# Moving a tile's scaling behind the branch and ending the routing two steps earlier in layer 1 of a two-layer expert kernel

## The chip, the cores and the metric

The kernel runs on one core of one Trainium2 chip. The metric is device time in microseconds of one execution, the median of the runs shown. Engines are named as in the profile: PE is the matrix engine (PEld its weight loads), DVE, ACT and POOL are the vector, scalar and general engines, SP issues most DMAs.

## The reference, cut to what matters

An attention block (4 x 8 heads, 576 rows, head width 64) gives 2304 token rows of width 512. Two mixture-of-experts layers follow, each with 8 experts of 512 x 1024 x 512.

```python
x = attention(q, k, v, M_prev, z_prev, beta)          # 2304 x 512
# layer 1: one expert a token
logits = x @ w_gate + modality_bias[modality_id]
e_idx = argmax(logits); gate_w = softmax(logits)[e_idx]
out[mask] = gate_w[mask] * (relu(x[mask] @ w1[e]) @ w2[e])     # per expert
# layer 2: two experts a token, chosen from the output of layer 1
logits = x @ w_gate; noise_scale = log1p(exp(x @ w_noise))
noisy = logits + noise_scale * noise
top2, w = two largest of noisy, softmax over the two
out[mask] += w * (relu(x[mask] @ w1[e]) @ w2[e])                # per expert, twice a token
```

What matters below: layer 2's choice of experts (the routing) needs each output row of layer 1, and layer 1's rows must be multiplied by the gate weight (the scaling) before they are routed.

## The kernel before, in words

**Units.** Layer 1 works in units of 256 rows (two tiles of 128) that share one expert. A unit of the common kind is written by `full` (line 791). The number of units is known only on the chip, so the last ones, and the units of half-filled experts written by `pair` (line 828), stand in nested `If` blocks (lines 780 and 785): the next block is entered by a branch that falls through, and when the count is reached all engines jump to the code behind all blocks. In this data unit 0 is done together with the attention, then come full unit 1, one pair, and full units 2 to 8, and then layer 2. So there are two jumps: from the pair to unit 2, and from unit 8 to layer 2.

**Slots.** A full unit has 16 slots. In slots 0 to 7 (loop variable f) `mm1` makes 128 of the 1024 hidden columns: 12 matmuls of 256 columns (lines 712 to 714: each fp32 value is split into a high and a low part, and three products are added). ACT then writes `hh`, DVE `hl`. In slots 8 to 15 (t and q, i=4t+q) `mm2` makes the two output tiles: four slots of six matmuls of 512 columns for each tile (lines 722 to 724).

**Work that rides along.** In slots 0 to 7 the second weight is split (`split_w`, line 685: ACT writes the high part `w2h`, POOL or DVE subtracts for the low part `w2l`). In slots 7 to 14 the next unit's first weight is split in the same way (`split_w1`, line 689, `w1h` and `w1l`; POOL has columns 0, 1, 3, 5, 7 and DVE 2, 4, 6). `rows` transposes the next unit's gathered rows on PE (line 702, tile `gs`). `logits` makes layer 2's logits of the unit before.

**The routing chain.** `route2` (line 868) is a generator of some 35 small operations, most on DVE, that routes the 256 rows of the unit before. `pump(slot)` issues PUMP of them. The chain yields 1 behind `A` (line 899), the one-hot sum of the two chosen experts: from there it is held until slot GATE[1], where PE counts the rows by five small matmuls of `A` (lines 901 to 905). Behind them DVE works out the places (`rk`, `W`, `r`, `ri`, `col`, `ol`, `oc`), POOL copies weights into `val` (line 920), and DVE forms `rrm` (line 928); there the chain yields 2 and its last matmuls wait until slot 1 of the next unit (`behind`).

**The end of a unit.** ACT scales output tile 0 behind slot 11 and output tile 1 behind slot 15 (line 827, in a pair line 861) into `x1`. `settle` issues what is left of the chain up to its second hold, and `kept` (line 771) has POOL copy two small tables for the next unit's routing. `x1_out` (line 865) writes both tiles to memory.

The order of instructions on each engine is that of the code: inside these loops nothing else reorders them, and each engine works in order.

Of the kernel before, what the change touches and what calls it, by code (L numbers as in the profile page):

```python
# [9 lines left out]
FT=mybir.dt.float32; FR=mybir.dt.float32r; I32=mybir.dt.int32  # L10
AF=mybir.ActivationFunctionType; OP=mybir.AluOpType; AX=mybir.AxisListType
# [272 lines left out]
NF=13; NH=8; NP2=NH//2; NSTAT=5; COLS=2*NF+NH; SLOTS=COLS*128  # L284
HC=4; FC=HC+NH
col=lambda u: 2*u if u<2 else FC+2*(u-2)
# [5 lines left out]

EARLY=256; CH=(C2-DEAD)//2
OLP=8
LSLOT=(0,1,3); GATE={1:12,2:99}; PUMP=5
LSLOT2=(0,1,3); GATE2={1:7,2:11}; PUMP2=8
AREAS=(9216,9216,5120,10240,8192,GB*XW,2*XW,512)

# [9 lines left out]
class Moe:  # L308
# [420 lines left out]
    def state(s):  # L729
        nc=s.nc; c=s.c  # L730
        s.run=c.tile([128,E],FT,name='run'); nc.gpsimd.memset(s.run,float(DEAD))
        s.M2=c.tile([128,4,NC2],FT,name='M2'); nc.gpsimd.memset(s.M2,0.0)

        s.NV=NF+NP2+1
        s.sv=c.tile([128,s.NV,2,4],FT,name='sv'); nc.gpsimd.memset(s.sv,8000.0)
        s.val=c.tile([128,s.NV,4,4],FT,name='val'); nc.gpsimd.memset(s.val,0.0)
        s.nz=c.tile([128,3,2,E],FT,name='nz')
        s.L=c.tile([128,2,2*E],FT,name='L'); s.nx=c.tile([128,2,2],FT,name='nx'); s.nxi=c.tile([128,2],I32,name='nxi'); s.lp=c.tile([128,UT],FT,name='lp')
        s.uxi=c.tile([128,2,NF],I32,name='uxi'); s.cnt=c.tile([128,2],I32,name='cnt')
        s.last=c.tile([128,NF],FT,name='last')  # L740
        s.gn=c.tile([128,NF,2],FT,name='gn'); s.gh=c.tile([128,NP2+1,2],FT,name='gh'); s.gni=c.tile([128,NF,2],I32,name='gni')
        s.gsi=c.tile([128,NP2+1,2],I32,name='gsi')
# [32 lines left out]
        G.tensor_copy(s.nz[:,2,:nt],s.nz[:,1,:nt])  # L775
    def layer1(s, w1, w2, wcat):
        nc=s.nc; tc=s.tc; s.wcat=wcat; wk=s.wk; ps=s.ps
        s.full(wk,ps,w1,w2,1)
        s.np=nc.values_load(s.cnt[0:1,1:2],min_val=0,max_val=NP2)
        with ExitStack() as deep:  # L780
            for p in range(NP2):
                deep.enter_context(tc.If(s.np>p)); s.pair(wk,ps,w1,w2,p)
        for u in range(2,NSTAT): s.full(wk,ps,w1,w2,u)
        s.nf=nc.values_load(s.cnt[0:1,0:1],min_val=1,max_val=NF-1)
        with ExitStack() as deep:  # L785
            for u in range(NSTAT,NF):
                deep.enter_context(tc.If(s.nf>u-1)); s.full(wk,ps,w1,w2,u)
    def behind(s):

        for _ in s.old: pass  # L790
    def settle(s):

        while s.hold!=2: s.pump(99,{1:0,2:0},1)
        s.old=s.chain
    def full(s, wk, ps, w1, w2, u):
        nc=s.nc; V=nc.vector
        e=s.expert(1,0) if u==1 else s.expert(0,u-1); s.load_w(s.w1r,w1,e)
        s.x1_out(s.np*2+2 if u==2 else col(u-1),2)
        s.chain=s.route2(wk,ps,u-1,2); s.hold=0
        nc.gpsimd.tensor_copy(s.nz[:,1],s.nz[:,0])  # L800
        for f in range(KF):
            s.mm1(ps,f,0,UT)
            if u==1: s.late(f)
            elif f==1: s.behind()
            if u>=NSTAT-1:
                if f==1:
                    last=s.last[:,u-1:u]
                    V.tensor_scalar(s.nx[:,0],s.M2[:,0,0:2],float(S0),0.0,op0=OP.add,op1=OP.max)
                    V.tensor_scalar(s.nx[:,1],s.nx[:,0],float(N),last,op0=OP.add,op1=OP.mult)
                    V.tensor_add(s.nxi,s.nx[:,1],s.gn[:,u-1])  # L810
                    V.tensor_scalar(s.run[:,0:1],last,float(EARLY),s.run[:,0:1],op0=OP.mult,op1=OP.max)
                if f==2: g=[s.gather(s.xd[:N+col(u-1)*128],s.nxi[:,t:t+1]) for t in range(2)]
            elif f==(7 if u==1 else 0): g=[s.gather(s.xd[:N],(s.gsi[:,0] if u==1 else s.gni[:,u-1])[:,t:t+1]) for t in range(2)]
            if f in LSLOT: s.logits(wk,ps,1+LSLOT.index(f))
            s.split_w(s.w2r,s.w2h,s.w2l,f,nc.vector if f in (3,5,7) else nc.gpsimd)
            if f>LSLOT[2]: s.pump(f)
            if f==7: s.split_w1(0,nc.gpsimd)
        s.load_w(s.w2r,w2,e)
        for t in range(2):
            for q in range(4):  # L820
                y=s.mm2(ps,t*128,range(2*q,2*q+2),y if q else None)
                i=4*t+q
                if i<7: s.split_w1(i+1,nc.vector if i%2 else nc.gpsimd)
                if i in ((3,5) if u==1 else (1,3)): s.rows(ps,i//4 if u==1 else i//2,g[i//4 if u==1 else i//2],s.xf[0] if u==1 else None)
                if t==1 and q==1: s.logits(wk,ps,0)
                s.pump(8+i)
            nc.scalar.activation(s.x1[:,t,:D],y,AF.Copy,scale=s.gws[:,col(u)+t:col(u)+t+1])
        s.settle()
        s.kept(col(u),2)
    def pair(s, wk, ps, w1, w2, p):  # L830


        nc=s.nc; V=nc.vector; G=nc.gpsimd; c0=HC+2*p
        e=s.expert(1,p+1); eb=s.expert(1,NP2+1+p)
        s.load_w(s.wb1,w1,eb)
        s.x1_out(c0-2,2)
        s.load_w(s.wb2,w2,eb)
        s.chain=s.route2(wk,ps,NF+p,2); s.hold=0
        G.tensor_copy(s.nz[:,1],s.nz[:,0])
        xf=s.xf[p%2]; g=[]  # L840
        for t,(a1,a2) in enumerate(((s.w1r,s.w2r),(s.wb1,s.wb2))):
            cs=slice(t*128,t*128+128)
            for q in range(4):
                if q%2==0: h=ps.tile([128,4,128],FT,name='h')
                for f in (2*q,2*q+1):
                    for k in range(KD): nc.tensor.matmul(h[:,f%4],a1[:,k,f*128:f*128+128],xf[:,k,cs],start=k==0,stop=k==KD-1)
                if q%2: nc.scalar.activation(s.hf[:,2*q-2:2*q+2,cs],h,AF.Relu)
                if t==0:
                    if q==1: s.behind(); g=[s.gather(s.xd[:N],s.gsi[:,p+1,j:j+1]) for j in range(2)]
                    if q in LSLOT: s.logits(wk,ps,1+LSLOT.index(q))  # L850
                if t or q>=LSLOT[2]: s.pump(8*t+q)
            if t==0: s.load_w(s.w1r,w1,e)
            y=ps.tile([128,512],FT,name='y')
            for q in range(4):
                for f in (2*q,2*q+1): nc.tensor.matmul(y,s.hf[:,f,cs],a2[:,f],start=f==0,stop=f==KF-1)
                if t:
                    for f in (2*q,2*q+1): s.split_w1(f,V if f%2 else G)
                elif q%2: s.rows(ps,q//2,g[q//2],s.xf[(p+1)%2])
                if t and q==0: s.logits(wk,ps,0)
                s.pump(8*t+4+q)  # L860
            nc.scalar.activation(s.x1[:,t,:D],y,AF.Copy,scale=s.gws[:,c0+t:c0+t+1])
            if t==0: s.load_w(s.w2r,w2,e)
        s.settle()
        s.kept(c0,2)
    def x1_out(s, c, n):
        d=s.xd[N:].rearrange('(c p) d -> p c d',p=128)
        s.nc.sync.dma_start(d[:,c:c+n] if isinstance(c,int) else d[:,bass.ds(c,n)],s.x1[:,:n])
# [90 lines left out]
    def layer2(s, w1, w2, out):  # L958


        nc=s.nc; tc=s.tc; V=nc.vector; NE=EARLY//128; wk=s.wk; ps=s.ps
        tb=s.new_tables('l2',NC2)
        s.hh,s.hl=s.hidden['l2']
        for h in (s.hh,s.hl): nc.gpsimd.memset(h[:,:,:DEAD].bitcast(FT),0.0)
        s.x1_out(s.nf*2+(FC-4),2)
        s.load_w(s.w1r,w1,E+1)
        s.chain=s.route2(wk,ps,NF+NP2,2); s.hold=0
        for f in range(KF):
# [6 lines left out]
        for t in range(NE):  # L975
            for q in range(4):
                y=s.mm2(ps,t*128,range(2*q,2*q+2),y if q else None)
# [13 lines left out]
        for e in range(E):  # L991
# [15 lines left out]
            for t in ts:  # L1007
                for q in range(2):
                    y=s.mm2(ps,t*128,range(4*q,4*q+4),y if q else None)
# [137 lines left out]
```

## Time and profile before

| | |
|---|---|
| median of 3 runs | 995.16 us (994.46 to 997.01) |
| profiled execution | 994.96 us, its span 993.2 us |
| PE busy | 949.5 us, 96% of the span |
| DVE, ACT, POOL busy | 57%, 49%, 36% |
| layer 1, units 1 to 8 with the pair | from 248.0 us to 508.5 us |

The span is the time from the first to the last instruction, so 1.8 us of the execution lie outside it. PE carries the kernel: what it stands idle in the middle is added to the time. In the rows further below, a row of the timeline has start, duration, engine, line, operation, result and operands, shape, count, and in brackets how long the engine stood idle before it and which engine ended that. The engines' names with a q (DVEq, POOLq) are their instruction queues, which handle semaphores and branches.

### The profile page before, as it was taken

How to read it: one execution, taken by the hardware profiler on the slowest of the kernel's cores; microseconds unless marked ns; L12 is line 12 of the kernel's file. 1: busy time of each engine (PE TensorE's matmuls, PEld its weight loads, DVE VectorE, ACT ScalarE, POOL GpSimd, SP SyncE). 2: the span in 40 equal slices, each digit the busy share in tenths (PEclk: the TensorE clock that was granted, in tenths of full speed). 3: DMA queues.
4: the chain of work that ended last, by engine and by line, in shares of the span. 5: the costliest groups of instructions: out<-in, count | busy, mean ns of one | idle time of the engine just before them, and what ended most of it. 6: DMA issues, size and time to landing. Idle time of an engine off the chain costs nothing. (4 is left out here: it accounts for less than half of the span.)

```text
span 993.2 us, 18544 instructions
## 1 busy us (share of the span) xinstructions
PE 949.5 (96%) x6849; PEld 835.0 (84%) x6849; DVE 568.4 (57%) x1675; ACT 487.7 (49%) x1141; POOL 352.8 (36%) x411
## 2 busy tenths in 40 slices
PE   7999999999998999999988999999999999999994
PEld 5888888888876888888867889898989989898983
DVE  8777776899853888888865344253342424244310
ACT  6887878784433555555532243343343434344320
POOL 4222232245634567666644311221313012131111
PEclk9999999999998999999989999999999999999998
DMA  7345856363585455556653334535546353534212
GB/s 208 97 113 186 264 190 194 113 228 101 158 310 186 154 207 195 177 192 210 213 174 128 87 106 135 131 76 135 142 105 153 111 121 106 160 77 110 29 23 35
DMA packets 83842, 144.99 MB, mean 146 GB/s; under 512 B 14480, under 2 KB 32912, under 8 KB 83728
## 3 DMA queue, kind: packets, MB, share of 16 engines
q1 hardware_dynamic: 73168, 117.10, 35.8%
q0 software_dynamic: 10560, 26.47, 13.5%
q8 instruction: 60, 0.98, 0.4%
q14 instruction: 54, 0.44, 0.1%
HBM read 111.65 MB, written 31.97 MB: 145 GB/s over the span
## 5 line engine op out<-in xcount | busy, mean ns | idle before, releaser
L712 PE MATMUL b<-xh,w1h 128*128 128x304 f32 (+3 forms) x800 | 242.1, 303 | 10.4 <-DVEq L785 4.7
L713 PE MATMUL b<-xl,w1h 128*128 128x304 f32 (+3 forms) x800 | 239.5, 299 | 2.8 <-DVEq L780 2.6
L714 PE MATMUL b<-xh,w1l 128*128 128x304 f32 (+3 forms) x800 | 238.6, 298 | 0.8 <-POOLq L780 0.8
L717 DVE SCALAR_TENSOR_TENSOR hl<-b,hh 128x304 fp32r<-128x304 f32 (+3 forms) x200 | 90.3, 452 | 215.2 <-ACT hh L715 215.2
L722 PE MATMUL b<-w2h,hh 128*128 128x512 f32 x464 | 189.1, 407 | 0.0
L724 PE MATMUL b<-w2h,hl 128*128 128x512 f32 x464 | 182.4, 393 | 0.0
L723 PE MATMUL b<-w2l,hh 128*128 128x512 f32 x464 | 181.9, 392 | 0.0
L955 POOL DMA_INDIRECT out_dram<-os,l2s x40 | 63.7, 1593 | 327.6 <-ACT os L954 248.9
L715 ACT ACTIVATE hh<-b 128x304 fp32r<-128x304 f32 (+3 forms) x200 | 81.8, 409 | 187.6 <-PE b L714 187.4
L712 PEld LDWEIGHTS b<-xh,w1h 128*128 128x128 f32 x800 | 153.8, 192 | 18.0 <-DVE hl L717 9.2
L713 PEld LDWEIGHTS b<-xl,w1h 128*128 128x128 f32 x800 | 154.1, 193 | 3.8 <-DVEq L780 2.8
L714 PEld LDWEIGHTS b<-xh,w1l 128*128 128x128 f32 x800 | 154.1, 193 | 1.1 <-POOLq L780 1.1
L724 PEld LDWEIGHTS b<-w2h,hl 128*128 128x128 f32 x464 | 87.6, 189 | 19.7
L723 PEld LDWEIGHTS b<-w2l,hh 128*128 128x128 f32 x464 | 88.2, 190 | 15.7
L722 PEld LDWEIGHTS b<-w2h,hh 128*128 128x128 f32 x464 | 88.0, 190 | 15.6
L151 ACT ACTIVATE p<-sm,l 128x128 f32<-128x128 f32 (+4 forms) x144 | 84.1, 592 | 17.2 <-DVE l L147 17.2
L687 ACT CAST w2h<-w2r 128x512 fp32r<-128x512 f32 x128 | 78.5, 613 | 0.0
L704 DVE TENSOR_TENSOR xl<-b,xh 128x512 fp32r<-128x512 f32 x56 | 38.4, 688 | 69.9 <-ACT xh L703 69.9
L703 ACT CAST xh<-b 128x512 fp32r<-128x512 f32 x56 | 32.8, 587 | 90.1 <-PE b L702 90.1
L954 ACT ACTIVATE os<-b,l2w 128x512 f32<-128x512 f32 x40 | 27.6, 691 | 99.3 <-PE b L724 46.6
L691 ACT CAST w1h<-w1r 128x512 fp32r<-128x512 f32 x128 | 74.7, 619 | 0.0
L692 POOL TENSOR_TENSOR w1l<-w1r,w1h 128x512 fp32r<-128x512 f32 x44 | 59.1, 1352 | 42.3 <-ACT w1h L691 41.2
(500 smaller groups left out, 1536.2 us busy)
## 6 DMA issues: line engine op xcount, KB each, us to landing
w1r<-in_w_dram SPq DMA_DIRECT2D x18, 2048.0 KB, 9.7
w2r<-in_w_dram SPq DMA_DIRECT2D x18, 2048.0 KB, 9.1
xd<-gs SPq DMA_DIRECT2D x24, 260.0 KB, 3.7
xd<-x SPq DMA_DIRECT2D x10, 520.0 KB, 10.1
out_dram<-gs SPq DMA_DIRECT2D x19, 256.0 KB, 3.8
k<-in_k_dram SPq DMA_DIRECT2D x16, 256.0 KB, 4.4
q<-in_q_dram SPq DMA_DIRECT2D x16, 256.0 KB, 3.7
v<-in_v_dram SPq DMA_DIRECT2D x16, 256.0 KB, 4.3
```

The lines of the kernel that those rows point to most:

```text
L151: s.nc.scalar.activation(s.P[b,i,u][:,lh*n:lh*n+n],s.SM[b,i,u][:,lh*n:lh*n+n],AF.Exp,scale=-1.0,bias=L[:,0,c:c+1],accum_out=L[:,1,c:c+1])
L687: nc.scalar.copy(hi[c],raw[:,c])
L691: nc.scalar.copy(s.w1h[:,:,fs],s.w1r[:,:,fs])
L712: nc.tensor.matmul(h[:,:n],s.w1h[:,k,fs],s.xh[:,k,cs],start=k==0,stop=False)
L713: nc.tensor.matmul(h[:,:n],s.w1h[:,k,fs],s.xl[:,k,cs],start=False,stop=False)
L714: nc.tensor.matmul(h[:,:n],s.w1l[:,k,fs],s.xh[:,k,cs],start=False,stop=k==KD-1)
L715: def mm1_a(s, h, f, c0, n): s.nc.scalar.activation(s.hh[:,f,c0:c0+n],h[:,:n],AF.Relu)
L717: cs=slice(c0,c0+n); s.nc.vector.scalar_tensor_tensor(s.hl[:,f,cs],h[:,:n],0.0,s.hh[:,f,cs].bitcast(FT),op0=OP.max,op1=OP.subtract)
L722: nc.tensor.matmul(y,s.hh[:,f,cs],s.w2h[f],start=f==0,stop=False)
L723: nc.tensor.matmul(y,s.hh[:,f,cs],s.w2l[f],start=False,stop=False)
L724: nc.tensor.matmul(y,s.hl[:,f,cs],s.w2h[f],start=False,stop=f==KF-1)
L955: nc.gpsimd.indirect_dma_start(out=out,out_offset=bass.IndirectOffsetOnAxis(ap=si[:,c:c+1],axis=0),in_=o,in_offset=None,compute_op=OP.add)
```

## The change

Five edits, all in layer 1. The numbers of the pump: GATE[1] goes from 12 to 10 and PUMP from 5 to 6, so that a full unit's chain reaches `A` in slot 7 instead of slot 8, counts on PE behind slot 10 instead of slot 12, and reaches its second hold in slot 12 instead of slot 14. The scaling of output tile 1 is no longer issued at the unit's end but by the new `finish` behind the branch, as ACT's first instruction of the next unit; it takes its gate weight from a copy `gwc` that POOL makes in slot 5. `kept` moves from the unit's end into slot 14. The two counts that the branches test are loaded into registers once, before unit 1.

```diff
@@ -292,7 +292,7 @@
 
 EARLY=256; CH=(C2-DEAD)//2
 OLP=8
-LSLOT=(0,1,3); GATE={1:12,2:99}; PUMP=5
+LSLOT=(0,1,3); GATE={1:10,2:99}; PUMP=6
 LSLOT2=(0,1,3); GATE2={1:7,2:11}; PUMP2=8
 AREAS=(9216,9216,5120,10240,8192,GB*XW,2*XW,512)
 
@@ -736,6 +736,7 @@
         s.val=c.tile([128,s.NV,4,4],FT,name='val'); nc.gpsimd.memset(s.val,0.0)
         s.nz=c.tile([128,3,2,E],FT,name='nz')
         s.L=c.tile([128,2,2*E],FT,name='L'); s.nx=c.tile([128,2,2],FT,name='nx'); s.nxi=c.tile([128,2],I32,name='nxi'); s.lp=c.tile([128,UT],FT,name='lp')
+        s.y=None; s.gwc=c.tile([128,1],FT,name='gwc')
         s.uxi=c.tile([128,2,NF],I32,name='uxi'); s.cnt=c.tile([128,2],I32,name='cnt')
         s.last=c.tile([128,NF],FT,name='last')
         s.gn=c.tile([128,NF,2],FT,name='gn'); s.gh=c.tile([128,NP2+1,2],FT,name='gh'); s.gni=c.tile([128,NF,2],I32,name='gni')
@@ -775,27 +776,30 @@
         G.tensor_copy(s.nz[:,2,:nt],s.nz[:,1,:nt])
     def layer1(s, w1, w2, wcat):
         nc=s.nc; tc=s.tc; s.wcat=wcat; wk=s.wk; ps=s.ps
+        s.np=nc.values_load(s.cnt[0:1,1:2],min_val=0,max_val=NP2)
+        s.nf=nc.values_load(s.cnt[0:1,0:1],min_val=1,max_val=NF-1)
         s.full(wk,ps,w1,w2,1)
-        s.np=nc.values_load(s.cnt[0:1,1:2],min_val=0,max_val=NP2)
         with ExitStack() as deep:
             for p in range(NP2):
                 deep.enter_context(tc.If(s.np>p)); s.pair(wk,ps,w1,w2,p)
         for u in range(2,NSTAT): s.full(wk,ps,w1,w2,u)
-        s.nf=nc.values_load(s.cnt[0:1,0:1],min_val=1,max_val=NF-1)
         with ExitStack() as deep:
             for u in range(NSTAT,NF):
                 deep.enter_context(tc.If(s.nf>u-1)); s.full(wk,ps,w1,w2,u)
+    def finish(s):
+
+        if s.y is not None: s.nc.scalar.activation(s.x1[:,1,:D],s.y,AF.Copy,scale=s.gwc)
     def behind(s):
 
         for _ in s.old: pass
-    def settle(s):
+    def settle(s, y):
 
         while s.hold!=2: s.pump(99,{1:0,2:0},1)
-        s.old=s.chain
+        s.old=s.chain; s.y=y
     def full(s, wk, ps, w1, w2, u):
         nc=s.nc; V=nc.vector
         e=s.expert(1,0) if u==1 else s.expert(0,u-1); s.load_w(s.w1r,w1,e)
-        s.x1_out(s.np*2+2 if u==2 else col(u-1),2)
+        s.finish(); s.x1_out(s.np*2+2 if u==2 else col(u-1),2)
         s.chain=s.route2(wk,ps,u-1,2); s.hold=0
         nc.gpsimd.tensor_copy(s.nz[:,1],s.nz[:,0])
         for f in range(KF):
@@ -814,6 +818,7 @@
             if f in LSLOT: s.logits(wk,ps,1+LSLOT.index(f))
             s.split_w(s.w2r,s.w2h,s.w2l,f,nc.vector if f in (3,5,7) else nc.gpsimd)
             if f>LSLOT[2]: s.pump(f)
+            if f==5: nc.gpsimd.tensor_copy(s.gwc,s.gws[:,col(u)+1:col(u)+2])
             if f==7: s.split_w1(0,nc.gpsimd)
         s.load_w(s.w2r,w2,e)
         for t in range(2):
@@ -824,16 +829,16 @@
                 if i in ((3,5) if u==1 else (1,3)): s.rows(ps,i//4 if u==1 else i//2,g[i//4 if u==1 else i//2],s.xf[0] if u==1 else None)
                 if t==1 and q==1: s.logits(wk,ps,0)
                 s.pump(8+i)
-            nc.scalar.activation(s.x1[:,t,:D],y,AF.Copy,scale=s.gws[:,col(u)+t:col(u)+t+1])
-        s.settle()
-        s.kept(col(u),2)
+                if i==6: s.kept(col(u),2)
+            if not t: nc.scalar.activation(s.x1[:,0,:D],y,AF.Copy,scale=s.gws[:,col(u):col(u)+1])
+        s.settle(y)
     def pair(s, wk, ps, w1, w2, p):
 
 
         nc=s.nc; V=nc.vector; G=nc.gpsimd; c0=HC+2*p
         e=s.expert(1,p+1); eb=s.expert(1,NP2+1+p)
         s.load_w(s.wb1,w1,eb)
-        s.x1_out(c0-2,2)
+        s.finish(); s.x1_out(c0-2,2)
         s.load_w(s.wb2,w2,eb)
         s.chain=s.route2(wk,ps,NF+p,2); s.hold=0
         G.tensor_copy(s.nz[:,1],s.nz[:,0])
@@ -858,10 +863,11 @@
                 elif q%2: s.rows(ps,q//2,g[q//2],s.xf[(p+1)%2])
                 if t and q==0: s.logits(wk,ps,0)
                 s.pump(8*t+4+q)
-            nc.scalar.activation(s.x1[:,t,:D],y,AF.Copy,scale=s.gws[:,c0+t:c0+t+1])
+                if not t and q==1: G.tensor_copy(s.gwc,s.gws[:,c0+1:c0+2])
+                if t and q==2: s.kept(c0,2)
+            if not t: nc.scalar.activation(s.x1[:,0,:D],y,AF.Copy,scale=s.gws[:,c0:c0+1])
             if t==0: s.load_w(s.w2r,w2,e)
-        s.settle()
-        s.kept(c0,2)
+        s.settle(y)
     def x1_out(s, c, n):
         d=s.xd[N:].rearrange('(c p) d -> p c d',p=128)
         s.nc.sync.dma_start(d[:,c:c+n] if isinstance(c,int) else d[:,bass.ds(c,n)],s.x1[:,:n])
@@ -962,7 +968,7 @@
         tb=s.new_tables('l2',NC2)
         s.hh,s.hl=s.hidden['l2']
         for h in (s.hh,s.hl): nc.gpsimd.memset(h[:,:,:DEAD].bitcast(FT),0.0)
-        s.x1_out(s.nf*2+(FC-4),2)
+        s.finish(); s.x1_out(s.nf*2+(FC-4),2)
         s.load_w(s.w1r,w1,E+1)
         s.chain=s.route2(wk,ps,NF+NP2,2); s.hold=0
         for f in range(KF):
```

DVE in slots 6 to 8 of unit 8, from the end of the polynomial (`acc`) to `A`; `mx` and `ix` are the two largest values and their indices, `id_` and `OH` the experts chosen. Before:

```order
L892 TENSOR_TENSOR n__6634<-acc,rg 128x16
L894 MAX mx_6636<-n__6634 128x8
L717 SCALAR_TENSOR_TENSOR hl_86<-b_156,hh_85 128x256
L688 TENSOR_TENSOR w2l_84<-w2r,w2h_76 128x512
L894 MAX mx_6636<-n__6634 128x8
L895 MAX_INDEX ix_6637<-mx_6636,n__6634 128x8 x2
L897 TENSOR_TENSOR id__6639<-ix_6637,tabs 128x4
L898 TENSOR_TENSOR OH<-io_175,id__6639 128x32
L899 TENSOR_TENSOR A_6673<-OH 128x16
```

and now:

```order
L897 SCALAR_TENSOR_TENSOR acc<-acc,qn 128x16
L898 TENSOR_TENSOR n__6647<-acc,rg 128x16
L900 MAX mx_6649<-n__6647 128x8 x2
L901 MAX_INDEX ix_6650<-mx_6649,n__6647 128x8 x2
L717 SCALAR_TENSOR_TENSOR hl_86<-b_156,hh_85 128x256
L688 TENSOR_TENSOR w2l_84<-w2r,w2h_76 128x512
L903 TENSOR_TENSOR id__6652<-ix_6650,tabs 128x4
L904 TENSOR_TENSOR OH<-io_175,id__6652 128x32
L905 TENSOR_TENSOR A_6675<-OH 128x16
```

The second MAX and the two MAX_INDEX now stand ahead of `hl` and the subtraction for `w2l`; `id_`, `OH` and `A` follow directly on `w2l`.

PE around the routing's count in unit 8; `b_157` and `b_158` are the banks of output tile 0 and 1. Before, behind the transposes of slot 11:

```order
L702 MATMUL b_159<-ident,gs_96 128x128 x4
L722 MATMUL b_158<-w2h_69,hh_85 128x512
L723 MATMUL b_158<-w2l_77,hh_85 128x512
L724 MATMUL b_158<-w2h_69,hl_86 128x512
L722 MATMUL b_158<-w2h_70,hh_85 128x512
L723 MATMUL b_158<-w2l_78,hh_85 128x512
L724 MATMUL b_158<-w2h_70,hl_86 128x512
L901 LDWEIGHTS trib
L901 MATMUL b_162<-A_6673,trib 128x8
```

and now, behind the transposes of slot 9:

```order
L702 MATMUL b_160<-ident,gs_100 128x128 x4
L722 MATMUL b_157<-w2h_73,hh_85 128x512
L723 MATMUL b_157<-w2l_81,hh_85 128x512
L724 MATMUL b_157<-w2h_73,hl_86 128x512
L722 MATMUL b_157<-w2h_74,hh_85 128x512
L723 MATMUL b_157<-w2l_82,hh_85 128x512
L724 MATMUL b_157<-w2h_74,hl_86 128x512
L907 LDWEIGHTS trib
L907 MATMUL b_162<-A_6675,trib 128x8
```

The count stood behind the first slot of tile 1 (slot 12), and stands now behind the third slot of tile 0 (slot 10).

DVE at the end of unit 8, up to the branch (`yt` is the copy of the transposed first output tile). Before:

```order
L923 SCALAR_TENSOR_TENSOR col<-ri,sv 128x4
L925 TENSOR_TENSOR ol_95<-io_175,ri 128x512
L927 TENSOR_TENSOR oc<-io_175,col 128x192
L928 TENSOR_TENSOR rrm<-oc,val 128x4x192
L785 COMPARE_AND_BRANCH
```

and now:

```order
L931 TENSOR_TENSOR ol_95<-io_175,ri 128x512
L933 TENSOR_TENSOR oc<-io_175,col 128x192
L934 TENSOR_TENSOR rrm<-oc,val 128x4x192
L692 TENSOR_TENSOR w1l<-w1r,w1h 128x4x128
L750 COPY yt<-b_160 128x4x128
L786 COMPARE_AND_BRANCH
```

`rrm` was the last instruction before the branch; a subtraction and the copy of `yt` now follow it.

## Rows read from the trace of the kernel before

**Rows 1.** Waits of PE: engine, line, awaited engine: us in total, times, longest

```profile
PE b L712 <- DVE hl L717: 4.1, 9, 0.9
PE b L901 <- DVE A L899: 2.7, 1, 2.7
PE b L465 <- DVE room L577: 1.5, 1, 1.5
```

**Rows 2.** Timeline of PE behind the pair's jump and behind unit 8's jump

```profile
312.92 0.39 PE L712 MATMUL b<-xh,w1h 128*128 128x256 f32 x1 [0.88 <-ACTq L780]
315.87 0.58 PE L713 MATMUL b<-xl,w1h 128*128 128x256 f32 x1 [2.56 <-DVEq L780]
317.24 0.58 PE L714 MATMUL b<-xh,w1l 128*128 128x256 f32 x1 [0.80 <-POOLq L780]
...
513.19 0.53 PE L712 MATMUL b<-xh,w1h 128*128 128x224 f32 x1 [4.71 <-DVEq L785]
```

**Rows 3.** Instructions of line 785, the branches: duration ns min/median/max, first and last start

```profile
L785 PEldq COMPARE_BRANCH x6: 65/80/5087, 396.8 to 510.1; - x6
L785 POOLq EVENT_SEMAPHORE x5: 17/43/43, 512.5 to 512.9; - x5
L785 DVEq EVENT_SEMAPHORE x1: 21/21/21, 513.0 to 513.0; - x1
```

**Rows 4.** Timeline of DVE in unit 8, around `A` and at the end

```profile
497.98 1.33 DVE L688 TENSOR_TENSOR w2l<-w2r,w2h 128x512 fp32r<-128x512 f32 x1
...
499.70 0.79 DVE L897 TENSOR_TENSOR id__6639<-ix,tabs 128x4 f32<-128x4 uint32 x1
...
500.75 1.15 DVE L899 TENSOR_TENSOR A<-OH 128x16 bf16<-128x16 f32 x1
...
509.58 1.99 DVE L928 TENSOR_TENSOR rrm<-oc,val 128x768 fp32r<-128x768 f32 x1 [0.35 <-POOL val L920]
```

**Rows 5.** Timeline of POOL in unit 8

```profile
497.48 3.00 POOL L692 TENSOR_TENSOR w1l<-w1r,w1h 128x512 fp32r<-128x512 f32 x2 [1.44 <-ACT w1h L691]
...
500.57 1.30 POOL L692 TENSOR_TENSOR w1l<-w1r,w1h 128x512 fp32r<-128x512 f32 x1
...
509.50 1.26 POOL L692 TENSOR_TENSOR w1l<-w1r,w1h 128x512 fp32r<-128x512 f32 x1
```

**Rows 6.** Timeline of PE in unit 8: slot 10's last matmul, the count

```profile
500.08 0.39 PE L724 MATMUL b<-w2h,hl 128*128 128x512 f32 x1
...
503.53 0.18 PE L901 MATMUL b<-A,trib 128*128 128x8 bf16 x1
```

**Rows 7.** Timeline of units 1 and 2: POOL and DVE, and slot 10's last matmul

```profile
268.19 3.80 POOL L692 TENSOR_TENSOR w1l<-w1r,w1h 128x512 fp32r<-128x512 f32 x3
...
268.42 3.61 DVE L897 TENSOR_TENSOR id__3371<-ix,tabs 128x4 f32<-128x4 uint32 x1
...
269.81 0.39 PE L724 MATMUL b<-w2h,hl 128*128 128x512 f32 x1
...
272.29 0.17 DVE L899 TENSOR_TENSOR A<-OH 128x16 bf16<-128x16 f32 x1
...
337.33 0.40 PE L724 MATMUL b<-w2h,hl 128*128 128x512 f32 x1
...
339.37 0.17 DVE L899 TENSOR_TENSOR A<-OH 128x16 bf16<-128x16 f32 x1
```

**Rows 8.** Timeline of POOL in the pair: its first subtraction for the next weight

```profile
305.74 1.27 POOL L692 TENSOR_TENSOR w1l<-w1r,w1h 128x512 fp32r<-128x512 f32 x1 [13.10 <-ACT w1h L691]
```

**Rows 9.** Stretches: us, busy time PE, PEld, DVE, ACT, POOL, granted clock, DMA, GB/s

```profile
230.00:240.00 10.00, 8.46 (x64) 7.34 (x63) 9.86 (x23) 4.10 (x10) 5.90 (x7) 1.00 0.00 0
317.00:322.00 5.00, 4.76 (x24) 4.76 (x25) 0.42 (x1) 1.49 (x3) 2.45 (x6) 0.56 0.73 233
513.00:518.00 5.00, 4.81 (x23) 4.84 (x24) 0.39 (x1) 1.40 (x3) 0.56 (x2) 0.50 0.64 169
533.00:538.00 5.00, 4.92 (x19) 3.98 (x19) 4.03 (x18) 0.20 (x1) 1.35 (x5) 0.66 0.53 135
```

## The prediction

> **What bounds the kernel now.** I read the waits of PE first, because PE carries the kernel, and in layer 1 they are few: short ones for `hl` inside the units, and one long one for `A` that lies in layer 2 [rows 1]. Then the timeline of PE at the two jumps. Behind the pair's jump PE stands 0.88, 2.56 and 0.80 us, each before one of the first three matmuls, awaiting ACT, DVE and POOL in turn, so 4.24 us; behind unit 8's jump it stands 4.71 us [rows 2]. The other branches are fallen through and cost PE nothing that I find. The change aims at these 8.95 us. Then I read DVE, POOL and PE side by side in units 1, 2 and 8, because the change pulls PE's count of the routing ahead, and PE works in order: a count that comes before its input stops all matmuls behind it.
>
> **What the waits at the jumps are.** At a jump each engine settles its semaphore before others may read it. In unit 8 PE's last matmul ends at 513.19 - 4.71 = 508.48. DVE starts `rrm` at 509.58 and ends it at 511.57 [rows 4]; its semaphore follows at 513.0, POOL's from 512.5 [rows 3], and PE goes on at 513.19. PE's own branch took up to 5.09 us [rows 3]: that one ends at about 509.8, 1.3 us behind its last matmul. So the jump cannot fall to nothing by making the other engines earlier.
>
> **Term 1, the count in slot 10: +14.4 us.** The chain's arithmetic gets no cheaper; PE's place moves. In unit 8 the count starts at 503.53, and `A` ends at 500.75 + 1.15 = 501.90: 1.6 us to spare. Slot 10's last matmul starts at 500.08, and its successor can start 0.23 us later, at 500.31 [rows 6]. If `A` ends when it does now, PE waits 501.90 - 500.31 = 1.6 us. Does PUMP=6 bring `A` forward? In the order, yes, by one slot. In time I think not. The value of `A` hangs on small DVE operations that stand blocked while POOL subtracts: `id_`, four columns, takes 0.79 us, and `A`, sixteen columns, 1.15 us, and `A` ends within 0.05 us of POOL's third subtraction at 500.57 + 1.30 = 501.87 [rows 4, 5]. The operations pulled ahead of `w2l` (a MAX and two MAX_INDEX, some 0.5 us) ran unblocked anyway; `w2l` itself waits for POOL's first subtraction in any case and ends at 499.31, whereupon POOL's second takes its turn until 500.48. `id_` then comes 0.46 us earlier into the same blockade, and `OH` and `A` into the next. So I leave `A` at 501.90. The bounds: had DVE the turn each time, `A` would end about 0.6 us behind `w2l`, at 499.9, and PE would not wait; if the addition `n` (line 892), which now ends just before POOL's first subtraction, slips behind it (the sixth operation of slot 4 stands before `hl` and pushes what follows by about 0.1 us), `A` comes some 0.5 us later, and PE waits 2.1 us. Units 4 to 8, five in all, repeat this pattern: 5 x 1.6 = 8.0.
>
> Units 2 and 3 gather earlier and share another pattern: slot 10 ends for PE at 337.33 + 0.23 = 337.56, `A` at 339.54 [rows 7]. Again `id_` meets a subtraction of POOL: 2 x 2.0 = 4.0 (bounds 0.7 and 2.0 each; the low one if `id_`, `OH` and `A` all run ahead of it).
>
> In unit 1 PE is ready at 269.81 + 0.23 = 270.04, and `A` ends at 272.46: 2.4. There `id_` took 3.61 us behind three subtractions in a row, of which two were issued after it [rows 7]. If the reordered `id_`, `OH` and `A` slip in before POOL's first, at about 268.2, PE waits for nothing: bounds 0 and 2.4, and I take the upper, since in the row POOL won three times.
>
> The Trainium skill, page "SBUF — State Buffer", section "Who interferes with whom", says that DVE and POOL share a port pair as an exclusive lock, and that whichever issues first gets it for the whole instruction. The blocked `id_` agrees with the lock, but not with the order of issue: POOL's second and third subtractions were issued after `id_` and went first. By the page's order `id_`, `OH` and `A` would each get a turn between POOL's subtractions in unit 1, `A` would end some 1 us earlier, and the forecast would be 1003 instead of 1004; I go by the row.
>
> The pair does not pay: its count moves into the first product, where `A` is some 5 us old. Layer 2 has its own numbers, which stay.
>
> **Term 2, the pair's jump: -3.0 us.** The scaling leaves ACT's path, and the routing ends before most of the weight split. What decides then is DVE and POOL fighting over the eight subtractions and `oc` and `rrm`. POOL's first starts at 305.74 and takes 1.27 [rows 8]. A subtraction of DVE, unblocked, is `w2l`'s end at 499.31 less the end of POOL's at 497.48 + 1.27: 0.56; `rrm` is 511.57 less 509.50 + 1.26: 0.8; `oc`, a quarter as wide, I put at 0.2 [rows 4, 5]. One at a time that is 4 x 1.27 + 4 x 0.56 + 1.0 = 8.3 us, to 314.0. PE's third matmul would start at 314.2 instead of 317.24 [rows 2]. Bounds: PE's last matmul ends at 312.04, and with 0.4 us for its branch the gain is at most 4.7; at least 0, if the ends only change places.
>
> **Term 3, unit 8's jump: -2.3 us.** DVE's last instruction becomes the copy of `yt`, whose input is there two slots before the end. But POOL now has two subtractions behind the routing's copies, where it had one [rows 5], so its semaphore, now 3.0 us behind the start of the last of them, does not move as far as DVE's. PE cannot go on before 1.3 us (its own branch) plus some 0.5 behind its last matmul. I take a gap of 2.4 between that 1.8 and 2.9 (DVE's 3.4 us from its last start to the semaphore, begun half a microsecond before PE ends): 4.71 - 2.4 = 2.3, with bounds 0 and 2.9.
>
> **Term 4, the clock: 0.** After the jumps the granted clock was 0.56 over 317 to 322 and 0.50 over 513 to 518, so 2.2 and 2.5 us lost and more behind; after the 2.7 us wait for `A` in layer 2 it was 0.66 over 533 to 538, 1.7 us lost; over 230 to 240, which holds a wait of 1.5 us (line 465), it stayed at 1.00 [rows 9, 1]. Between 1.2 and 2.4 GHz a fall therefore costs about 1.7 us or more. The jumps, cut to some 2.5 us, should each still bring one short fall: about 1.8 saved in all. Unit 1's wait of 2.4 is nearer to 2.7 and brings one; those of 1.6 and 2.0 are nearer to 1.5 and bring none: 1.7 lost. Bounds: -5 (no fall at all) and +12 (a fall at every wait).
>
> **The rest: 0.** The scaling moved behind the branch is still ACT's next instruction and waits for the same matmul; the write of `x1` behind it, the logits of tile 1 in slot 0 and SP's weight load are queued behind it as before. POOL's copy of `gwc` (0.2 us) falls where POOL waits for ACT. The two register loads before unit 1 run while PE has queued matmuls; SP's weight load for unit 1 is some 1.3 us later and is not needed for 10 us. The `hl` waits of some 0.5 us a unit lie before `A` and vanish into the wait for it.
>
> **Sum.** 14.4 - 3.0 - 2.3 = +9.1 on the profiled 994.96 us, which lies 0.2 below the median of 995.16: 1004.1, so 1004 us. Its own range is 1000.5 to 1008.
>
> **Rivals.**
> - `A` comes in time (0.15). POOL gets no turn between `w2l` and `A`, because these three now follow it without a gap. For it: `A` needs only 0.6 us of unblocked work. Against it: POOL had a turn there in every unit I read. Then only terms 2 and 3 are left, and the clock's part of up to 2: 988 to 990, faster.
> - `A` comes in time in some units only, or halves the wait (0.10): -7 from term 1, 997.
> - The waits let the clock fall (0.12): 1.7 us at each of five to seven waits, 1004 + 8.5 to 12, so 1012 to 1016. For it: a 2.7 us wait did; against it: 1.5 did not.
> - The change does not do what it says (0.08): POOL or the jump itself keeps both gaps as long as now, and terms 2 and 3 vanish: 1009.
>
> **How the numbers follow.** The forecast has 0.55. From 991 to 1013 no more than 2 in 10 is left out: the first rival and the upper end of the third. Within 0.3% means 992.2 to 998.1 here, about what a measurement of this kernel can tell from no change. Faster than that holds the first rival, 0.15, and a little of the second: 0.16. Same takes most of the second: 0.08. Slower is the rest: 0.76.
>
> **What would show it.** In the profile after, the waits of PE should hold a line of the count for `A` with eight waits and some 14 us; the timeline of unit 8 should show `A` ending with POOL's third subtraction, and PE idle before the count. Behind the jumps the idle of PE should be about 2.5 us each, and the granted clock in the units 1.00. If PE's waits for `A` are absent, term 1 is wrong and the first rival holds; if the clock falls inside the units, the third.

## The result and the profile after

The changed kernel takes 1003.48 us (median of 6 runs, 998.64 to 1003.97), the kernel before beside it 994.81 us: a ratio of 1.0071, 95% interval 1.0047 to 1.0096. It is slower by 0.7%; the prediction was 1004 us.

The profiled execution is the one of 998.64 us, the quickest of the six, with a span of 996.8 us. The first lines of its page (span, then busy us, share of the span and instructions of each engine):

```profile
span 996.8 us, 18555 instructions
PE 945.7 (95%) x6849; PEld 831.7 (83%) x6849; DVE 561.9 (56%) x1675; ACT 487.9 (49%) x1141; POOL 359.9 (36%) x420
```

Span less PE's busy time is what PE stood: 993.2 - 949.5 = 43.7 us before, 51.1 us now, so 7.4 us more. PE's busy time fell by 3.8 us with the same 6849 matmuls, because the clock was granted more often in this execution (mean 0.988, against 0.983 before). The other five runs have 0.982 to 0.985. How they differ is told with the changed kernel's second profile, below.

The waits of PE in the changed kernel, which answer to [rows 1] and [rows 2] (the columns are those of rows 1; lines from 739 on have moved down by up to 6):

```profile
PE b L907 <- DVE A L905: 15.3, 9, 2.7
...
PE b L712 <- DVE hl L717: 5.7, 8, 0.8
...
PE b L713 <- DVEq L782: 1.1, 1, 1.1
...
PE b L712 <- DVEq L786: 0.7, 1, 0.7
...
PE b L712 <- PEq L782: 0.5, 1, 0.5
...
PE b L714 <- POOLq L786: 0.2, 1, 0.2
```

Nine waits for `A` instead of one: eight new ones, 15.3 - 2.7 = 12.6 us. The `hl` waits rose from 4.1 to 5.7. At the pair's jump 0.5 + 1.1 = 1.6 us are left of 4.24, at unit 8's 0.7 and a piece of 0.2 of 4.71. So +12.6 + 1.6 - 2.6 - 3.8 = 7.8, against the 7.4 that the page gives.

Unit 8 around the count, PE, then DVE, then POOL, to be held beside [rows 4 to 6]:

```profile
510.17 0.40 PE L724 MATMUL b<-w2h,hl 128*128 128x512 f32 x1
512.02 0.17 PE L907 MATMUL b<-A,trib 128*128 128x8 bf16 x1 [1.45 <-DVE A L905]
```

```profile
508.33 1.08 DVE L688 TENSOR_TENSOR w2l<-w2r,w2h 128x512 fp32r<-128x512 f32 x1
509.34 1.25 DVE L903 TENSOR_TENSOR id__6652<-ix,tabs 128x4 f32<-128x4 uint32 x1
510.62 0.19 DVE L904 TENSOR_TENSOR OH<-io,id__6652 128x32 f32<-128x32 f32 x1
510.85 1.12 DVE L905 TENSOR_TENSOR A<-OH 128x16 bf16<-128x16 f32 x1
```

```profile
507.57 3.00 POOL L692 TENSOR_TENSOR w1l<-w1r,w1h 128x512 fp32r<-128x512 f32 x2 [1.59 <-ACT w1h L691]
...
510.66 1.28 POOL L692 TENSOR_TENSOR w1l<-w1r,w1h 128x512 fp32r<-128x512 f32 x1
...
515.96 0.19 POOL L926 CAST wh<-w__6723 128x4 fp32r<-128x4 f32 x1 [3.34 <-DVE w__6723 L925]
```

`id_`, four columns, takes 1.25 us beside POOL's second subtraction, `A` 1.12 us beside the third, and `A` ends at 511.97, 0.03 us after POOL's 511.94. That is the picture of [rows 4, 5], with the count now in front of it. (The last row, POOL idle for 3.34 us behind the count, is used further below.)

The jumps, PE behind the pair and behind unit 8:

```profile
316.00 0.38 PE L712 MATMUL b<-xh,w1h 128*128 128x256 f32 x1 [0.50 <-PEq L782]
317.51 0.48 PE L713 MATMUL b<-xl,w1h 128*128 128x256 f32 x1 [1.13 <-DVEq L782]
...
520.90 0.34 PE L712 MATMUL b<-xh,w1h 128*128 128x224 f32 x1 [0.74 <-DVEq L786]
```

And the stretches ahead of unit 1's wait, behind it, over units 2 to 7, and around unit 8's jump (columns as in rows 9):

```profile
262.00:268.00 6.00, 5.79 (x27) 5.32 (x28) 5.69 (x29) 2.27 (x5) 2.84 (x3) 0.72 0.02 6
272.00:278.00 6.00, 5.27 (x23) 4.29 (x23) 3.62 (x17) 1.66 (x4) 0.40 (x3) 0.72 0.81 291
322.00:500.00 178.00, 165.26 (x1140) 145.76 (x1139) 131.45 (x368) 93.89 (x200) 118.60 (x152) 1.00 0.55 184
516.00:524.00 8.00, 7.05 (x45) 5.86 (x44) 4.70 (x8) 2.67 (x6) 5.81 (x11) 1.00 0.24 86
```

The clock had fallen once ahead of unit 1's wait (0.72 over 262 to 268), as it did before (0.72 there too), and fell again behind it; it stayed at 1.00 (2.4 GHz) over the waits of units 2 to 7, and did not fall at unit 8's jump, where it had been 0.50 [rows 9].

### The profile page after: what moved, and what is told of

It is laid out like the page before. It is cut to its first block, busy times and chain, and to the rows that moved or that the text cites. A ratio compares the mean times of both kernels' runs of the same rounds, so it can differ in the third digit from the quotient of the medians.

```text
span 996.8 us, 18555 instructions
## 1 busy us (share of the span) xinstructions
PE 945.7 (95%) x6849; PEld 831.7 (83%) x6849; DVE 561.9 (56%) x1675; ACT 487.9 (49%) x1141; POOL 359.9 (36%) x420
## 5 line engine op out<-in xcount | busy, mean ns | idle before, releaser
L692 DVE TENSOR_TENSOR w1l<-w1r,w1h 128x512 fp32r<-128x512 f32 x84 | 67.4, 811 | 18.4 <-ACT w1h L691 18.2
L692 POOL TENSOR_TENSOR w1l<-w1r,w1h 128x512 fp32r<-128x512 f32 x44 | 69.4, 1593 | 13.1 <-ACT w1h L691 11.7
```

The lines of the kernel that those rows point to most:

```text
L692: eng.tensor_sub(s.w1l[:,:,fs],s.w1r[:,:,fs],s.w1h[:,:,fs].bitcast(FT))
```

## The experiments

Theory W: PE's waits for `A` are the loss, and the jumps give some of it back. Theory P, on what makes `A` late: POOL's subtractions between `w2l` and `A`. The runs came in three groups, each on one chip and with its own runs of the kernel before (medians): 998.03 us for the first four, 997.74 for the next four, 996.13 for the last two. Ratios are to these; the absolute times expected of the first four were reckoned from 995 us.

### The count put back to slot 12

```diff
-LSLOT=(0,1,3); GATE={1:10,2:99}; PUMP=6
+LSLOT=(0,1,3); GATE={1:12,2:99}; PUMP=6
```

> The changed kernel with the count put back to slot 12 (PUMP stays 6, scaling and the other edits stay). Theory W (the waits of PE for A in slot 10 are the whole loss): the eight waits for A in layer 1 (12.6 us with the change) vanish, the jumps keep most of their 6.6 us, so 986 to 990 us. Rival R (the loss is not the waits, but the moved scaling, the earlier chain or the clock by itself): 998 to 1004 us.

997.76 us, ratio 1.0002 (0.9992 to 1.0012). Its waits:

```profile
PE b L712 <- DVE hl L717: 6.0, 9, 0.8
PE b L712 <- DVEq L786: 4.2, 1, 4.2
PE b L713 <- DVEq L782: 2.9, 1, 2.9
PE b L907 <- DVE A L905: 2.7, 1, 2.7
...
PE b L714 <- POOLq L782: 1.0, 1, 1.0
```

All eight waits for `A` in layer 1 are gone, and with them the loss: that half of W holds. But I expected a gain of 5 to 9 us, and there is none: the jumps are back at 4.2 us and, with 0.4 for PE's own queue, 4.4 us. I had taken the waits and the gains for separate terms. They hang on one number: the routing's `rrm` ends early only if the count is early.

### The numbers of the pump alone

```diff
-LSLOT=(0,1,3); GATE={1:12,2:99}; PUMP=5
+LSLOT=(0,1,3); GATE={1:10,2:99}; PUMP=6
```

(on the kernel before, nothing else)

> The kernel before with GATE 10 and PUMP 6 alone; scaling, kept and register loads as before. Theory W: eight waits for A with 12 to 13 us in all, as with the whole change. At unit 8's jump rrm is early, so the gap falls from 4.7 to 1 to 3 us whatever the scaling does; at the pair's jump too. 1002 to 1007 us. Rival R (the moved scaling causes the loss): 987 to 995 us.

1009.04 us, ratio 1.0117 (1.0099 to 1.0134), by the ratios some 5 us worse than the whole change, and at the upper end of what I expected if that is reckoned from this group's 998 us. The eight waits come to 14.2 us instead of 12 to 13, because unit 1 waited 4.0 us here. The scaling of tile 1 still stands before the branch, and PE's waits are:

```profile
PE b L901 <- DVE A L899: 16.9, 9, 4.0
PE b L712 <- DVE hl L717: 6.9, 10, 0.9
PE b L712 <- ACTq L785: 3.4, 1, 3.4
```

With `rrm` early, ACT ends the wait at unit 8's jump: 3.4 us, more than the 1 to 3 us that I expected "whatever the scaling does", against 0.7 and 0.2 in the changed kernel. So the moved scaling is worth some 2.5 us there, once the routing is out of the way. At the pair's jump 0.9 (ACT) and 0.8 us (DVE) are left, as much as in the changed kernel.

### The moved scaling alone

```diff
-LSLOT=(0,1,3); GATE={1:10,2:99}; PUMP=6
+LSLOT=(0,1,3); GATE={1:12,2:99}; PUMP=5
```

(on the changed kernel)

> The changed kernel with GATE 12 and PUMP 5: only the scaling behind the branch, kept in slot 14 and the early register loads are left of the change. Theory W: no waits for A in layer 1; rrm is DVE's last instruction before the branch again, so unit 8's gap stays at 4 to 4.7 us; the pair's gap may lose ACT's 0.9 us: 993 to 995.5 us. Rival S (the scaling is what held up the jump): gap of unit 8 below 2 us, 988 to 991 us.

996.59 us, ratio 0.9982 (0.9969 to 0.9995). Unit 8's gap stays at 4.5 us, for DVE; theory S falls. At the pair's jump 0.4 + 3.0 + 1.0 = 4.4 us are left, so the scaling alone gains nothing at the jumps; the numbers alone, in the run above, gained 2.6 us at the pair's and 1.3 at unit 8's, and the last 2.5 at unit 8's take both. Against the run with slot 12 only PUMP differs: with 5 the `hl` waits of PE are 4.2 instead of 6.0 us, and the median is 1.2 us less, about what these runs can tell.

### The count in slot 11

```diff
-LSLOT=(0,1,3); GATE={1:10,2:99}; PUMP=6
+LSLOT=(0,1,3); GATE={1:11,2:99}; PUMP=6
```

> The changed kernel with the count in slot 11. Theory W: PE reaches the count some 1.4 us or more later than in slot 10, where it waited 1.45 us, so waits of 0 to 0.1 us in units 2 to 8 and about 1 us in unit 1; routing still ends early enough: 986 to 990 us, the same as with slot 12 or up to 1 us less. Rival B (POOL's turns move A along with the count): 0.5 to 1 us a unit is left, 992 to 997 us.

997.75 us, ratio 0.9997 (0.9984 to 1.001), not the gain expected. Waits for `A`: 4.5 us in all, so 1.8 in unit 1 beside layer 2's 2.7, and none in units 2 to 8. The gap at unit 8's jump is 3.2 us, at the pair's 0.4 + 1.9 + 1.0. Each slot that the count is moved ahead takes about 1 to 2.5 us off unit 8's gap (4.2, 3.2, 0.7 for slots 12, 11 and 10), and only the last slot costs waits in units 2 to 8. So 2.3 us are gained at the jumps and 1.8 lost in unit 1; the `hl` waits are 6.2 instead of 4.1 us, and this profile has a wait of 2.1 us for gathered rows in layer 2 (line 702) that no other has.

### POOL's subtractions moved behind the count in the program

```diff
-                if i<7: s.split_w1(i+1,nc.vector if i%2 else nc.gpsimd)
+                if i<7: s.split_w1(i+1,nc.vector if i%2 else nc.gpsimd,i in (0,2))
                 s.pump(8+i)
+                if i==2:
+                    for f in (1,3): s.low(f,nc.gpsimd)
```

(`split_w1` with a third argument issues ACT's cast alone, and `low` the subtraction)

> The changed kernel, but POOL's subtractions for columns 1 and 3 of the next weight are issued behind the count of slot 10 (ACT's casts stay where they are). Theory P (POOL's turns between w2l and A are what makes A late): A ends some 0.5 us before PE reaches the count, the waits for A in layer 1 fall from 12.6 us to under 1.5 us, the jumps stay at 0.7 to 2 us each; with before at 998 us here, less 6 us of the jumps, plus 1.6 us for hl, less up to 2 us of clock: 990 to 994 us. Rival V (DVE's own chain makes A late): the waits stay at 1.2 us or more a unit, 1003 to 1007 us.

1004.15 us, ratio 1.0065 (1.0045 to 1.0085), and 15.4 us of waits for `A`, as in the changed kernel (15.3). By the expectation rival V wins, but the trace says otherwise. DVE, then POOL, in unit 8:

```profile
511.09 0.15 DVE L908 TENSOR_TENSOR id__6652<-ix,tabs 128x4 f32<-128x4 uint32 x1
511.27 1.24 DVE L909 TENSOR_TENSOR OH<-io,id__6652 128x32 f32<-128x32 f32 x1
512.55 1.17 DVE L910 TENSOR_TENSOR A<-OH 128x16 bf16<-128x16 f32 x1
```

```profile
511.18 2.51 POOL L695 TENSOR_TENSOR w1l<-w1r,w1h 128x512 fp32r<-128x512 f32 x2
```

POOL did not wait for PE's count, since nothing makes it wait: both subtractions started at 511.18, as soon as POOL was free, and `id_`, now unblocked, made way for `OH`, which was blocked in its place. `A` again ends with POOL's last, at 513.7. The blockade had not been taken away, so the run decides nothing between P and V.

### The same with fewer operations in slots 4, 6 and 7

```diff
-            if f>LSLOT[2]: s.pump(f)
+            if f>LSLOT[2]: s.pump(f,n=6 if f==5 else 5)
```

> As the run with POOL's two subtractions moved, and besides PUMP is 5 in slots 4, 6 and 7 and 6 only in slot 5, just enough for A to be reached in slot 7. Theory H (the sixth operation of slot 4 is what lengthens the hl waits from 0.5 to 0.8 us in units 4 to 8): these waits fall back to about 0.5 us, 1.2 to 1.6 us less than the run without this edit: 988.5 to 992.5 us. Rival: the waits stay at 0.8 us and the two runs take the same time.

1007.87 us, ratio 1.0106 (1.0085 to 1.0127). Theory H holds for the `hl` waits:

```profile
PE b L912 <- DVE A L910: 17.6, 9, 3.0
...
PE b L715 <- DVE hl L720: 4.2, 9, 0.8
```

4.2 us, as with PUMP 5. But `A` did not come earlier with `hl`: in units 4 to 8 PE waits 0.52 us for `hl` and 1.68 for `A`, against 0.79 and 1.45 in the run above, 2.2 us a unit either way. The run was even 3.7 us slower. In the profiled executions, 4.6 us apart in span, PE's standing makes 1.1 of it (span less busy 53.1 against 52.0), which is a wait in the attention (line 465, 1.6 us instead of 0.4). The other 3.5 us are busy time, and so the clock. Unit 5's count, and the stretches behind the counts of units 4 and 5, in this run (unit 6's is like them, 0.59):

```profile
429.10 0.17 PE L912 MATMUL b<-A,trib 128*128 128x8 bf16 x1 [1.70 <-DVE A L910]
```

```profile
399.00:403.00 4.00, 4.00 (x14) 3.23 (x14) 2.33 (x10) 1.43 (x4) 0.00 (x0) 0.57 1.01 371
430.00:434.00 4.00, 4.00 (x14) 3.22 (x13) 2.65 (x14) 2.39 (x6) 0.03 (x1) 0.57 0.94 363
```

Behind three of the seven waits of 1.7 to 1.8 us in units 2 to 8 the granted clock was 0.57 to 0.59, near its lower level (1.2 GHz), and 4.00 of 4.00 us busy did fewer matmuls.

### The changed kernel and the kernel before once more

> The changed kernel as it is, beside the kernel before on this chip. Theory W: eight waits for A of 12 to 13 us in all, ratio to before 1.006 to 1.009, so 1004 to 1007 us. Where its own executions differ by 5 us: theory C says that the clock falls at some of the waits of 1.45 us inside units 2 to 8; rival S says that the difference lies in the attention, in a stall of ACT near 221 us (2.1 us of PE's time and one or two short falls of the clock behind it) that the runs with the count in slots 11 and 12 show and the first profile of the changed kernel does not; then the clock in units 2 to 8 is 1.00 in the slow executions as well.

> The kernel before as it is, one look on this chip. Theory S: an execution of 997 us or more has ACT's stall near 221 us and clock 0.983 or lower; one of 995 us or less has not. Rival: the executions near 998 us have no such stall, and the difference to the first chip's 995 us lies elsewhere.

The changed kernel: 1003.42 us (1002.08 to 1007.17), ratio 1.0058 (1.0037 to 1.0079). Its profiled execution took 1004.42 us, a usual one, and is 5.9 us longer in span than the first profile (1002.7 against 996.8). The stretches near 222 us, ahead of unit 1's count and behind it, and over units 2 to 8:

```profile
222.00:226.00 4.00, 3.98 (x21) 3.98 (x22) 3.60 (x10) 3.05 (x7) 1.49 (x1) 0.57 0.42 138
262.00:268.00 6.00, 5.08 (x36) 4.66 (x36) 5.73 (x23) 3.20 (x9) 1.51 (x3) 1.00 0.02 4
273.00:281.00 8.00, 6.52 (x23) 5.24 (x23) 5.26 (x20) 2.54 (x6) 1.90 (x4) 0.57 0.70 244
325.00:530.00 205.00, 189.05 (x1296) 165.90 (x1295) 151.38 (x421) 107.03 (x227) 135.39 (x176) 1.00 0.53 181
```

Theory C falls for this kernel: over units 2 to 8 with their waits of 1.4 to 1.5 us the clock is 1.00 here too. What is there instead is a stall of 1.5 us in the attention with a fall of the clock behind it, and a wait of 4.0 us for `A` in unit 1 (2.5 in the first profile) with a longer fall. Ahead of that wait the clock was 1.00 here and 0.72 in the first profile, which by my estimate takes 1.7 us of PE's time from those 6. PE was ready for the count 2.0 us behind the end of `w2l` there and 0.4 us here, and so waited less there. The kernel before, 998.77 us, has the stall in the attention as well (2.2 us), and the first profile of before, of 994.96 us, has not: two executions of each kernel agree with theory S. Between the two of the kernel before PE stands 1.5 us more (the wait for `room`, line 465, is 1.2 us shorter where the stall came before it) and is busy 2.4 us longer. The copy for which PE stands there, on ACT, in the run with slot 12 and in the first profile of before:

```profile
223.09 0.37 ACT L186 COPY oc<-b 128x256 f32<-128x256 f32 x1 [2.23 <-remote]
```

```profile
220.29 0.37 ACT L186 COPY oc<-b 128x256 f32<-128x256 f32 x1 [0.24 <-PE b L167]
```

Eight of twelve profiles have this stall, in code that the change does not touch, the kernel before among them. Its cause I leave open. It makes executions of one kernel differ, and does not tell the kernels apart.

### POOL held until `A` is done

```diff
-        A=T('A2',SH,BF); V.tensor_add(A,OH[:,0],OH[:,1]); yield 1
+        A=T('A2',SH,BF); V.tensor_add(A,OH[:,0],OH[:,1]); s.A2=A; yield 1
...
                 if i==2:
+                    nc.gpsimd.tensor_copy(s.seen,s.A2[:,0,0:1])
                     for f in (1,3): s.low(f,nc.gpsimd)
```

(on top of the run with the two subtractions moved)

> As the run with POOL's two subtractions moved, but now POOL is made to wait for A before them: a copy of one column of A into a spare tile stands ahead of them, so they cannot start before A is done. Theory P (POOL's turns make A late): A ends within 0.7 us of w2l's end, before PE reaches the count, the waits for A in units 2 to 8 are below 0.2 us, the jumps stay at 0.7 to 2 us each, and with before at 997.8 us on this chip the time is 990 to 994 us (ratio 0.992 to 0.996). Rival V (DVE's own chain): the waits stay at 1.2 us or more, 1002 to 1006 us.

987.51 us, ratio 0.991 (0.9895 to 0.9926). Unit 8, DVE, POOL and PE:

```profile
496.39 1.09 DVE L688 TENSOR_TENSOR w2l<-w2r,w2h 128x512 fp32r<-128x512 f32 x1
497.41 0.15 DVE L909 TENSOR_TENSOR id__6660<-ix,tabs 128x4 f32<-128x4 uint32 x1
497.59 0.19 DVE L910 TENSOR_TENSOR OH<-io,id__6660 128x32 f32<-128x32 f32 x1
497.82 0.17 DVE L911 TENSOR_TENSOR A<-OH 128x16 bf16<-128x16 f32 x1
```

```profile
498.06 0.58 POOL L836 CAST seen<-A 128x1 f32<-128x1 bf16 x1 [0.52 <-DVE A L911]
498.60 2.53 POOL L695 TENSOR_TENSOR w1l<-w1r,w1h 128x512 fp32r<-128x512 f32 x2
```

```profile
498.24 0.40 PE L727 MATMUL b<-w2h,hl 128*128 128x512 f32 x1
498.48 0.18 PE L913 MATMUL b<-A,trib 128*128 128x8 bf16 x1
```

`id_`, `OH` and `A` take 0.15, 0.19 and 0.17 us, `A` is done 0.6 us behind `w2l`, and PE goes from slot 10 into the count without a pause. Theory P is shown: same operations, same order on DVE, only POOL's turn taken away, and the ratio goes from 1.0065 in the run with the two subtractions moved to 0.991, just below the 0.992 to 0.996 that I expected. In units 2 to 8 no wait for `A` is left; in unit 1 1.6 us. POOL's deferred work fitted where POOL had stood idle for 3.34 us in the changed kernel, waiting for DVE's `W`; 1.48 us of that wait are left here.

### Both together

> As the run in which POOL is held until A, with PUMP 5 in slots 4, 6 and 7 and 6 in slot 5. Theory P and theory H together: the hl waits in units 4 to 8 are 0.5 us instead of 0.8 us, and the MAX_INDEX operations behind w2l cost nothing, since they run unblocked before PE is at the count: 988.5 to 992.5 us, 1 to 1.5 us less than the run without this edit. If the waits for A come back (over 0.3 us a unit), the two operations behind w2l are too many.

987.35 us, ratio 0.9911 (0.9898 to 0.9925), the same as the run before it within either interval. The waits for `hl` did fall, 5.7 to 3.8 us, those for `A` from 4.3 to 3.7, with one of 0.4 us in unit 2 and none in units 3 to 8; the gain of 1 to 1.5 us that I expected is not to be seen. In these two profiles PE stands 2.4 us less here, but is busy 2.0 us longer, at a mean clock of 0.985 instead of 0.988; whether the clock takes the gain in the other executions too is open. Both are some 0.9% faster than the kernel before, and by the ratios 1.5% faster than the changed one.

## Why the prediction was right, and where not

**Term 1 (+14.4).** Right in mechanism and nearly in size: 12.6 us. Units 4 to 8 waited 1.45 us each instead of 1.6, units 2 and 3 1.41 and 1.45 instead of 2.0, unit 1 2.49 instead of 2.4 (in the second profile 4.0, and 14.1 in all). That POOL's subtractions hold `A`, read from ends that fell together within 0.05 us, is what the held run showed. The first rival, `A` in time because its operations follow `w2l` without a gap, failed for the reason given against it: POOL took its turn each time.

Unit 1 again differs from the order of issue:

```profile
268.20 4.04 DVE L903 TENSOR_TENSOR id__3401<-ix,tabs 128x4 f32<-128x4 uint32 x1
```

```profile
268.48 3.74 POOL L692 TENSOR_TENSOR w1l<-w1r,w1h 128x512 fp32r<-128x512 f32 x3
```

`id_` began ahead of all three subtractions, while POOL still issued a DMA (267.50 to 268.45), and was passed by them. The Trainium skill, page "SBUF — State Buffer", section "Who interferes with whom", has an exclusive pair that DVE shares with GpSimd when its two inputs lie in SBUF; the held run agrees, where `id_` took 0.15 us. That issue order decides who blocks, as it also says, the row contradicts once more.

**Term 2 (-3.0).** 1.63 us left of 4.24: -2.6. Right, and DVE's part is the larger one left (1.13). Only its upper bound, 4.7, was more than the 4.24 that PE stood there.

**Term 3 (-2.3).** The step "PE cannot go on before 1.3 us (its own branch) plus some 0.5 behind its last matmul" failed. The gap fell to 0.74 + 0.2, so by some 3.8 us. PE's longest branch took 5.09 us before [rows 3], and now:

```profile
L786 PEldq COMPARE_BRANCH  x6: 65/80/3518, 401.2 to 520.4; - x6
L786 DVEq EVENT_SEMAPHORE  x1: 21/21/21, 520.7 to 520.7; - x1
```

I had taken one execution's 5.09 us for a property of the jump. PE's own semaphore, which follows that branch, came 1.4 us behind its last matmul before, and in the changed kernel as that matmul ended (520.2). The other side of the gap failed as well: DVE's 3.4 us from its last start to its semaphore became 0.7 (`yt` starts at 519.99). PE's branch took 5.1 and 5.2 us in the runs with POOL held, and there the gap was 2.0 us; in the first of them it was PE's own queue that ended it:

```profile
L789 PEldq COMPARE_BRANCH  x6: 65/80/5118, 394.1 to 508.3; - x6
```

So the floor that I named exists in some programs and not in others; what sets the length is open. The Trainium skill, page "Runtime: NRT & Kernel Launch", section "Instruction fetch mechanics", says that a taken branch to code that is not loaded must first fetch it. That the four fall-throughs take 65 to 90 ns and the jump microseconds agrees (the sixth, 0.19 us, starts behind PE's semaphore); no run here shows the fetch itself.

**Term 4 (0).** The 0 holds in sum in the second profile, where PE is busy 949.4 us against 949.5 before, and not in the first, where it is 3.8 us less. Of the places, the pair's jump (0.79 over 314 to 322) and unit 1's wait were followed by a fall as forecast; unit 8's jump was not, nor were the waits of 1.4 to 1.5 us in units 2 to 8. In the run with waits of 1.7 to 1.8 us there, 0.25 us longer, three of seven were. So the rival of the falling clock was near.

**The rest (0).** The `hl` waits did not stay at 0.5 us: they grew to 0.8 in units 4 to 8, and from 4.1 to 5.7 in all, since the sixth operation of slot 4, which I had seen standing before `hl`, delays it (0.52 us in the runs with five operations there). That they "vanish into the wait" for `A` held: an `hl` that comes late makes PE late at the count by as much, and the wait for `A` is shorter, as the run with fewer operations shows, 2.2 us a unit either way. So this +1.6 nearly replaces the 1.8 that term 1 had too much.

**The sum.** With each term at its measured size in the first profile, 12.6 + 1.6 - 2.6 - 3.8 = 7.8, it gives 1002.8 on 994.96; that execution took 998.64, because its clock gave 3.8 us back. In the second profile, a usual execution, the terms are 14.1 + 1.9 - 2.6 - 3.8 = 9.6, so 1004.6, and it took 1004.42. The 1004 of the prediction was right with errors that partly cancelled. A part of it is luck: beside the 994.81 us of the first comparison the change adds 8.7 us, beside the 997.74 of the second 5.7. The forecast of 9.1 us, or 0.9%, lies inside the first interval (0.47 to 0.96%) and a little above the second (0.37 to 0.79%).

**What I did not see:** that terms 1, 2 and 3 are one. A count in slot 12 or 11 costs nothing in units 2 to 8 and gains little at the jumps; slot 10 gains 6.4 and costs 12.6; with POOL held 5.3 of the gain stay, and 1.6 us of the cost, in unit 1.

## What to carry to other kernels

When a small operation takes five to eight times its usual time and ends with a large one of another engine, the large one is the cost of moving its reader ahead: price the move by that end, and look for idle time of the other engine behind the reader. To move work out of the way, a place later in the program is not enough; the engine must be made to wait for what it is to let pass. A wait that is short on its own can still cost the clock, so look at the granted clock behind it, and not in one execution only.

## What the runs showed of the hardware

- Waits of PE of 1.40 to 1.47 us, seven in each of four profiles, were never followed by a fall of the granted clock; of seven of 1.7 to 1.8 us in one profile three were, and unit 1's single waits of 1.6 and 1.8 us in two others were not. Those of 2.5 to 4.0 us in unit 1 were, in all five profiles that have one.
- Of three dependent DVE operations of 0.15 to 0.19 us each, two took 1.1 to 1.25 us beside subtractions of POOL, in the changed kernel and with the subtractions moved, and none did once POOL was made to wait for the third.
- PE's taken branch between unit 8 and layer 2 took 3.5 to 3.7 us in the four programs that waited for `A` in slot 10, and 4.6 to 5.2 us in the others. The cause is open.
- ACT stalled by 1.5 to 2.2 us near 221 us in eight of twelve profiles, in front of one and the same copy; the profile names "remote" as its releaser in six of them, and in two a matmul of line 419 that had ended 1 us before. The cause is open.
